# Wider moving operands for two kinds of narrow TensorE products in an attention stage

## The chip, the cores and the metric

The kernel runs on one core of one Trainium2 chip. The metric is the device time of one execution in microseconds. All times and counts below come from the times of the kernel before, from the page of its profile or from an answer of its trace.

## What is computed

Three parts follow one another. An xLSTM-like attention with input, forget and output gates runs over 4 batches, 8 heads, 768 tokens and a head size of 40. Its result, rows of 320 numbers for 3072 tokens, goes to a router that gives each token to one of 8 experts, 384 tokens each. Each expert is a two-layer product with ReLU, followed by a gated product common to all. Cut to what matters here:

```
for t in range(S):                       # attention, per batch and head
    m_new = max(f[t] + m, i[t])
    C = exp(f[t] + m - m_new) * C + exp(i[t] - m_new) * outer(v[t], k[t])
    n = exp(f[t] + m - m_new) * n + exp(i[t] - m_new) * k[t];  m = m_new
    y[t] = sigmoid(o[t]) * (C @ q[t]) / max(abs(n @ q[t]), 1)
logits = x @ w_gate                      # x: 3072 x 320, w_gate: 320 x 8
# tokens to experts by the order of the logits, 384 to each; then
h = relu(x[mask] @ w1[e]); out[mask] = h @ w2[e]
y = (sigmoid(x @ wg) * (x @ wv)) @ wo
```

## The kernel before

The attention is done in 6 chunks of 128 tokens. In a chunk the 32 pairs of batch and head are taken in three sets of 12, 12 and 8 heads. So there are 18 steps j (chunk c = j // 3, set s = j % 3). All products of this stage are in float32, apart from the decays. In the trace a float32 product has two matmul records and two weight loads, a transpose one of each.

The work of a step, by method:

- `trans` transposes queries and keys, 3 heads at a time (line 211); ScalarE copies them out.
- `decay` forms the logarithm of the decay matrix of 4 heads: one bfloat16 product of 512 columns that writes all of a PSUM tile (line 235), then four of 128 columns, each into its quarter of the same tile (line 237). ScalarE takes the exponential (line 241) into `ee`.
- `score` forms keys times queries, 128 columns for each head (line 250), and VectorE multiplies `ee` by them.
- `outp` multiplies these weights by the values: for each head the weights (128 x 128) are loaded as the stationary operand and the head's 41 columns (40 values and a one) are streamed (line 297). The results of all heads of the step stand side by side in one PSUM tile `po`, 41 columns each.
- `inter` and `state` read and renew the running state, three heads at a time with 123 columns (lines 261 and 280). `comb` adds the parts (line 307).
- `flip` transposes the finished rows of two batches (line 341), and `lmm` multiplies them by the router's weights: five accumulated products of 16 columns each (line 354), of which VectorE copies the 16 logits of each token out (`half2`, line 359).

Around this, VectorE, ScalarE, GpSimd and the DMA queue unpack the weights of the last part (`prep_moe2`, lines 745 to 796), from step 2 on. The program gives the stage in the order of the list `ORDER`, but the order of each engine's instructions is then settled by a planner that works with estimated costs of the instructions, so that products of neighbouring steps stand between each other. Behind the attention that planner is off, and the order is the program's.

The router starts when the last logits are there (line 606 is its first product). The experts follow; there TensorE works without pause.

Of the kernel before, what the change touches and what calls it, by code (L numbers as in the profile page):

```python
# [7 lines left out]
FT = mybir.dt.float32  # L8
# [13 lines left out]
L = 128  # L22
# [3 lines left out]
E = 8  # L26
# [4 lines left out]
GK = (3, 3, 2)  # L31
# [9 lines left out]
class Attention:  # L41
# [248 lines left out]
    def outp(self, j, k):  # L290
        nc = self.nc
        s = j % NS
        if k == 0:
            self.PO[j] = self.ps.tile([L, HS, 41], FT, name="po", bufs=1)
        w = self.W.pop((j, k))
        for h in range(4):
            nc.tensor.matmul(self.PO[j][:, 4 * k + h, :], w[:, h, :], self.VN[s][:, 4 * k + h, :], start=True, stop=True)  # L297

    def comb(self, j):
        nc = self.nc  # L300
# [48 lines left out]

    def lmm(self, c, z, i0, n):  # L350
        if i0 == 0:
            self.PL = self.ps.tile([L, 2, E], FT, name="pic", bufs=1)
        for i in range(i0, i0 + n):
            self.nc.tensor.matmul(self.PL, self.XT[c, z][:, i, :], self.wgt[:, i], start=(i == 0), stop=(i == 4))

    def half2(self, c, z, i0=0):
        self.lmm(c, z, i0, 5 - i0)
        lg = self.g["lg"].rearrange("p (b c) e -> p b c e", c=NC)
        self.nc.vector.tensor_copy(lg[:, 2 * z:2 * z + 2, c, :], self.PL)

    def run(self, rt, fn):
        rt.consts(self.one)
# [828 lines left out]
```

## Time and profile before

| | |
|---|---|
| median of 3 runs | 876.02 us (875.86 to 878.23) |
| the profiled execution | 875.33 us |
| its span, first to last instruction | 873.4 us |
| time around the span | 1.93 us |
| TensorE: matmuls busy, weight loads busy | 827.8 us (95%), 788.4 us (90%) |
| VectorE, ScalarE, GpSimd busy | 535.7 us, 377.7 us, 229.0 us |
| mean granted TensorE clock | 0.958 |

The page shows each engine's busy time, then the span in 40 slices with the granted clock of TensorE (1.00 is 2.4 GHz, 0.50 is 1.2 GHz), then the chain of work that ended last and the costliest groups of instructions. Matmuls are pipelined: a run of them that begin 0.1 us apart and last 0.28 us each shows TensorE as busy throughout, so a busy share near 1 does not tell how fast it works. For that, the length of a run of products is to be read against their number.

### The profile page before, as it was taken

Reading aid. Unit: us, or ns where it says so; the run is one execution under the profiler, and the core shown is the slowest. Engines: PE = TensorE matmul, PEld = TensorE weight load, DVE = VectorE, ACT = ScalarE, POOL = GpSimd, SP = SyncE. Lnnn points to the kernel's source line nnn. Section 1 sums busy time; section 2 is a strip of 40 time slices with the busy share of each in tenths; the row PEclk is TensorE's granted clock in tenths of the full one; section 3 lists DMA queues with packets and bytes.
Section 4 is the critical chain, followed back from the end, with each engine's and each line's share of the span. In section 5 each row is a group of like instructions: output and inputs, shape, how many; then the busy total and the mean of one; then the engine's idle time right before and its main releaser. Section 6 shows DMA issues by size and latency. Waiting matters only on the chain.

```text
span 873.4 us, 16420 instructions
## 1 busy us (share of the span) xinstructions
PE 827.8 (95%) x6332; PEld 788.4 (90%) x6332; DVE 535.7 (61%) x1442; ACT 377.7 (43%) x827; POOL 229.0 (26%) x235
## 2 busy tenths in 40 slices
PE   6899898997499999999999999999999999999996
PEld 5899897996299999999999999999999999999996
DVE  8668787875666666565565666566565665643321
ACT  6798889660043252252225134322522342252321
POOL 1125343430120081063017104400810360062001
PEclk9799999897599999999999999999999999999998
DMA  7997786620130230050040005002200500140000
GB/s 131 164 233 176 190 190 155 154 59 31 59 98 1 69 88 24 13 145 23 1 131 26 23 2 156 23 2 78 79 23 2 146 33 2 38 118 23 1 1 24
DMA packets 124574, 64.07 MB, mean 73 GB/s; under 512 B 103760, under 2 KB 115216, under 8 KB 124496
## 3 DMA queue, kind: packets, MB, share of 16 engines
q1 hardware_dynamic: 122048, 55.10, 25.7%
q0 software_dynamic: 2304, 7.87, 2.8%
q8 instruction: 50, 0.82, 0.4%
q14 instruction: 28, 0.23, 0.1%
q10 hardware_dynamic: 144, 0.05, 0.0%
HBM read 55.14 MB, written 7.86 MB: 72 GB/s over the span
## 4 chain that ended last, share of the span: by engine, by line
PE 71%; DVE 2%; DMA 1%; ACT 1%; issue 1%; POOL 0%; POOLq 0%; DVEq 0%; ACTq 0%
PE mm L974 8%; PE mm L975 8%; PE mm L996 8%; PE mm L976 8%; PE ac L1090 5%; PE mm L981 5%; PE mm L980 5%; PE ac L1092 5%; PE ac L1091 5%; PE rp L606 3%; PE ac L1013 3%; PE ac L1015 2%; PE ac L1014 2%; PE ac L1019 1%; PE ac L1018 1%; DMA xg<-xd,ix 1%
## 5 line engine op out<-in xcount | busy, mean ns | idle before, releaser
L974 PE MATMUL mm<-yh,mh 128*128 128x384 f32 x384 | 134.1, 349 | 0.0
L975 PE MATMUL mm<-yh,ml 128*128 128x384 f32 x384 | 129.1, 336 | 0.0
L976 PE MATMUL mm<-yl,mh 128*128 128x384 f32 x384 | 129.1, 336 | 0.0
L934 POOL DMA_INDIRECT xg<-xd,ix x24 | 24.0, 1000 | 376.3 <-DVE scr L701 371.4
L1069 ACT ACTIVATE sg<-mm 128x384 f32<-128x384 f32 x96 | 47.2, 492 | 132.9 <-PE mm L981 132.9
L1076 DVE TENSOR_TENSOR gl<-gf,gh 128x384 fp32r<-128x384 f32 x96 | 77.5, 807 | 37.1 <-ACT gh L1082 36.9
L1082 ACT ACTIVATE gh<-gf 128x384 fp32r<-128x384 f32 x96 | 50.2, 523 | 114.6 <-DVE gf L1081 114.6
L1090 PE MATMUL ac<-oh,gh 128*128 128x320 f32 x288 | 92.6, 321 | 0.0
L1092 PE MATMUL ac<-oh,gl 128*128 128x320 f32 x288 | 89.2, 310 | 0.7 <-DVE gl L1076 0.7
L1091 PE MATMUL ac<-ol,gh 128*128 128x320 f32 x288 | 89.1, 310 | 0.0
L1081 DVE TENSOR_TENSOR gf<-sg,mm 128x384 f32<-128x384 f32 x96 | 52.6, 548 | 52.6 <-ACT sg L1069 52.0
L1004 ACT ACTIVATE gh<-mm 128x384 fp32r<-128x384 f32 x64 | 31.3, 491 | 118.2 <-PE ac L1019 52.8
L974 PEld LDWEIGHTS mm<-yh,mh 128*128 128x128 f32 x384 | 72.4, 189 | 0.2 <-DVE xl L915 0.2
L975 PEld LDWEIGHTS mm<-yh,ml 128*128 128x128 f32 x384 | 72.6, 189 | 0.0
L976 PEld LDWEIGHTS mm<-yl,mh 128*128 128x128 f32 x384 | 72.2, 188 | 0.0
L981 PE MATMUL mm<-pad,mr 128*128 128x384 f32 x192 | 64.7, 337 | 0.0
L980 PE MATMUL mm<-y,m 128*128 128x384 f32 x192 | 64.5, 336 | 0.0
L250 PE MATMUL s<-qT,kb 120*128 120x128 f32 x384 | 59.6, 305 | 3.1 <-ACT kb L219 2.1
L250 PEld LDWEIGHTS s<-qT,kb 120*128 120x128 f32 x384 | 54.1, 216 | 4.5 <-ACT kb L219 2.9
L241 ACT ACTIVATE ee<-pg,GT 128x128 f32<-128x128 f32 x192 | 54.5, 391 | 3.5 <-PE po L297 1.6
L1092 PEld LDWEIGHTS ac<-oh,gl 128*128 128x128 f32 x288 | 54.1, 188 | 0.9 <-DVE gl L1076 0.9
L1090 PEld LDWEIGHTS ac<-oh,gh 128*128 128x128 f32 x288 | 54.5, 189 | 0.0
(287 smaller groups left out, 1990.6 us busy)
## 6 DMA issues: line engine op xcount, KB each, us to landing
ws<-in_moe_w_dram SPq DMA_DIRECT2D x15, 480.0 KB, 6.7
ws<-in_moe_w_dram SPq DMA_DIRECT2D x14, 512.0 KB, 4.1
ws<-in_moe_w_dram SPq DMA_DIRECT2D x18, 256.0 KB, 5.4
on<-in_o_gate_dram SPq DMA_DIRECT2D x24, 160.0 KB, 3.8
xd<-y SPq DMA_DIRECT2D x24, 160.0 KB, 2.5
st<-in_moe_w_out_dram SPq DMA_DIRECT2D x12, 320.0 KB, 3.6
st<-in_moe_w_gate_dram SPq DMA_DIRECT2D x8, 384.0 KB, 4.3
st<-in_moe_w_val_dram SPq DMA_DIRECT2D x8, 384.0 KB, 4.2
```

The costliest lines, as they stand in the source:

```text
L241: nc.scalar.activation(ee[:, h, :], pg[:, h, :], AF.Exp, bias=self.GT[:, c, h0 + h:h0 + h + 1])
L250: nc.tensor.matmul(s[:, h, :], self.KB[:, a, r, :], self.QT[j][:, a, :], start=True, stop=True)
L974: mm(p, wh[:, d, cs], h[:, d], start=(d == 0), stop=False)
L975: mm(p, wl[:, d, cs], h[:, d], start=False, stop=False)
L976: mm(p, wh[:, d, cs], l[:, d], start=False, stop=False)
L980: mm(p, w2[:, cs], x[2], start=False, stop=False)
L981: mm(p, wr[:, c2], self.pad[z], start=False, stop=True)
L996: mm(p, (self.al if t == 1 else self.ah)[:, d, cs], x[t // 2][:, d], start=(d == 0 and t == 0), stop=False)
L1076: nc.vector.tensor_tensor(gl, hs[f - 1][0], hs[f - 1][1].bitcast(FT), op=OP.subtract)
L1090: mm(o, gh[:, ts], self.oh[:, k], start=(k == 0), stop=False)
L1091: mm(o, gh[:, ts], self.ol[:, k], start=False, stop=False)
L1092: mm(o, gl[:, ts], self.oh[:, k], start=False, stop=(k == 11))
```

## The change

In `outp`, each head's weights are multiplied not by that head's 41 columns but by up to three heads' (123 columns; 82 and 41 for the last two heads of a step). The columns of the next heads are written with products that nobody wants, and the next heads' own products, which come after them, write over them. In `lmm`, the 16 columns of the router's weights are streamed seven times (112 columns, by an access with step 0) into a PSUM tile seven times as wide, of which the copy reads the first 16 columns. The number of instructions stays.

```diff
         w = self.W.pop((j, k))
         for h in range(4):
-            nc.tensor.matmul(self.PO[j][:, 4 * k + h, :], w[:, h, :], self.VN[s][:, 4 * k + h, :], start=True, stop=True)
+            hh = slice(4 * k + h, min(4 * k + h + 3, 4 * GK[s]))
+            nc.tensor.matmul(self.PO[j][:, hh, :], w[:, h, :], self.VN[s][:, hh, :], start=True, stop=True)
...
     def lmm(self, c, z, i0, n):
         if i0 == 0:
-            self.PL = self.ps.tile([L, 2, E], FT, name="pic", bufs=1)
+            self.PL = self.ps.tile([L, 7, 2, E], FT, name="pic", bufs=1)
         for i in range(i0, i0 + n):
-            self.nc.tensor.matmul(self.PL, self.XT[c, z][:, i, :], self.wgt[:, i], start=(i == 0), stop=(i == 4))
+            self.nc.tensor.matmul(self.PL, self.XT[c, z][:, i, :], self.wgt[:, i][:, None].to_broadcast([L, 7, 2, E]),
+                                  start=(i == 0), stop=(i == 4))
...
-        self.nc.vector.tensor_copy(lg[:, 2 * z:2 * z + 2, c, :], self.PL)
+        self.nc.vector.tensor_copy(lg[:, 2 * z:2 * z + 2, c, :], self.PL[:, 0])
```

## Rows read from the trace of the kernel before

**Rows 1.** The page, 40 slices of the span: TensorE's busy tenths, its granted clock.

```profile
PE   6899898997499999999999999999999999999996
...
PEclk9799999897599999999999999999999999999998
```

**Rows 2.** Stretches: us, PE, PEld, DVE, ACT, POOL busy (instructions), PEclk, DMA, GB/s.

```profile
33.00:212.00 179.00, 169.25 (x1377) 160.21 (x1377) 132.75 (x289) 137.64 (x370) 63.91 (x65) 0.90 0.68 155
...
236.50:873.40 636.90, 624.75 (x4617) 601.56 (x4617) 357.14 (x978) 216.12 (x404) 156.39 (x147) 0.99 0.16 49
```

**Rows 3.** The same view: the stretches of the attention at the lower clock.

```profile
17.98:21.39 3.41, 3.14 (x17) 2.51 (x17) 3.38 (x8) 3.34 (x11) 0.00 (x0) 0.50 0.30 36
31.64:41.88 10.24, 8.89 (x45) 8.69 (x46) 3.30 (x6) 6.84 (x20) 2.11 (x2) 0.50 1.02 172
65.77:69.18 3.41, 3.41 (x20) 3.07 (x19) 0.74 (x4) 3.39 (x7) 0.98 (x1) 0.50 0.85 237
89.66:93.08 3.42, 3.42 (x18) 3.42 (x18) 1.46 (x3) 3.38 (x12) 2.17 (x3) 0.50 0.83 175
120.38:123.80 3.42, 3.42 (x18) 3.42 (x18) 1.44 (x4) 3.38 (x11) 1.00 (x1) 0.50 1.00 208
147.69:151.10 3.41, 3.41 (x16) 3.25 (x17) 1.96 (x5) 3.41 (x12) 0.26 (x1) 0.50 1.04 225
168.17:175.00 6.83, 6.83 (x34) 6.83 (x34) 6.56 (x17) 2.55 (x9) 2.99 (x3) 0.50 0.56 171
205.72:211.54 5.82, 5.43 (x26) 5.19 (x27) 0.81 (x4) 1.12 (x4) 0.07 (x1) 0.50 0.24 86
```

**Rows 4.** Timeline, TensorE ahead of falls: start, length, line, tiles, shape, count.

```profile
63.79 1.96 PE L297 MATMUL po<-vn,ee 128*128 128x41 f32 x16
...
116.97 2.77 PE L297 MATMUL po<-vn,ee 128*128 128x41 f32 x24
...
164.64 1.88 PE L297 MATMUL po<-vn,ee 128*128 128x41 f32 x16
...
166.70 1.19 PE L354 MATMUL pic<-wgt,xt 128*128 128x16 f32 x10
```

**Rows 5.** Timeline, TensorE after waits (in brackets: idle before, and who ended it).

```profile
32.99 0.90 PE L211 MATMUL tr<-ident,qn 128*120 128x128 f32 x3 [2.30 <-ACT GT L175]
...
88.28 0.49 PE L250 MATMUL s<-qT,kb 120*128 120x128 f32 x2 [0.78 <-ACT kb L219]
...
147.57 1.80 PE L250 MATMUL s<-qT,kb 120*128 120x128 f32 x6 [1.36 <-ACT kb L219]
...
205.85 0.40 PE L354 MATMUL pic<-wgt,xt 128*128 128x16 f32 x1 [0.64 <-ACT xt L342]
```

**Rows 6.** Timeline, VectorE waiting for TensorE at the lower clock.

```profile
36.12 0.67 DVE L310 COPY t<-po 128x492 f32<-128x492 f32 x1 [3.27 <-PE po L297]
...
69.16 0.67 DVE L263 TENSOR_TENSOR t<-pic,GT 128x492 f32<-128x492 f32 x1 [2.67 <-PE pic L261]
...
211.31 0.17 DVE L359 COPY lg<-pic 128x16 f32<-128x16 f32 x1 [2.61 <-PE pic L354]
```

**Rows 7.** Timeline, TensorE: runs of products of different widths, at either clock.

```profile
34.32 1.77 PE L297 MATMUL po<-vn,ee 128*128 128x41 f32 x8
...
42.73 1.04 PE L297 MATMUL po<-vn,ee 128*128 128x41 f32 x8
...
102.09 1.05 PE L261 MATMUL pic<-cs,qT 120*128 120x123 f32 x8
...
175.20 0.38 PE L235 MATMUL pg<-negi,tris 128*128 128x512 bf16 x1
175.42 0.39 PE L237 MATMUL pg<-GB,sel 96*128 96x128 bf16 x4
```

**Rows 8.** Groups, 33 to 212 us: line, engine, shape, count, busy us, mean ns, idle before.

```profile
L297 PE MATMUL po<-vn,ee 128*128 128x41 f32 x344 | 43.5, 281 | 0.1
L261 PE MATMUL pic<-cs,qT 120*128 120x123 f32 x110 | 17.4, 307 | 0.5 <-DVE lg L359 0.5
```

## The prediction, made before the result was known

> **What bounds the kernel now.** I read the slices first, then stretches of the span, then single runs of TensorE. In the slices TensorE is busy nearly throughout, and its granted clock dips again and again in the first ten slices and hardly later [rows 1]. The change touches only the attention, which ends at 212 us; from 236.5 us on the clock is 0.99 [rows 2] and nothing is changed there. In the attention's main part, 33 to 212 us, TensorE shows 169 of 179 us busy, VectorE 133 and ScalarE 138, at a mean clock of 0.90 [rows 2]. So TensorE is the most loaded engine there, and it works part of the time at half rate.
>
> Where, the eight stretches at 0.50 (1.2 GHz) tell [rows 3]. TensorE was busy in them for 3.14 + 8.89 + 3.41 + 3.42 + 3.42 + 3.41 + 6.83 + 5.43 = 38.0 us. That the rate really halves is seen on the same products: eight records of line 297 take 1.77 us at the lower level and 1.04 us at the upper [rows 7]; without the last one's own length (about 0.4 and 0.28 us) they begin 0.20 and 0.11 us apart. So about half of 38.0 us, 19 us, is what the lower level costs TensorE. That TensorE is what others wait for in these stretches shows on VectorE, which stood idle for 3.27, 2.67 and 2.61 us behind it there [rows 6].
>
> What came ahead of the falls is of two kinds. Ahead of those at 65.77, 120.38 and 168.17 us TensorE never paused, but it issued long runs of the narrow products: 16, 24 and 16 records of 41 columns, and ten of 16 columns [rows 4]. Ahead of those at 89.66 and 147.69 us it had waited for ScalarE's copies of the keys, 0.78 and 1.36 us [rows 5]. The falls at 31.64 and 205.72 us had both: 16 narrow records right before, and a wait (2.30 and 0.64 us) beside [rows 5]. The one at 17.98 us lies in the stage's start.
>
> **The change part by part.** *More columns in the same number of products.* A run of 41 columns and one of 123 columns take the same at the upper level: 1.04 us for eight of line 297, 1.05 us for eight of line 261 [rows 7]. Each record stands on its own load of 128 stationary columns, and that load sets the distance of 0.11 us. So 82 more columns at line 297 and 96 more at line 354 lie under a load that is there already; I cost them at nothing. If that cover were gone: 512 bfloat16 columns take 0.22 us from one start to the next [rows 7], 0.43 ns a column, and a float32 product has two records, so 0.86 ns. Added are 6 x (2 x (10 x 82 + 41) + 6 x 82 + 41) = 13,530 columns of values and 60 x 96 = 5,760 of logits, together 19,290 columns or 16.6 us. The row of 123 columns is of the very width, so I take zero and keep 16.6 us for a rival.
>
> The Trainium skill, page "TensorE: Matmul & The Clock Gate", section "Back-to-back issue gap", speaks against this change: there the spacing of matmuls grows with the columns streamed. By that rule alone the added columns would lengthen every product, and the sum would be worse by the 16.6 us; lines 297 and 261 differ by a factor of three in columns and not in pace, so this trace goes by the load instead.
>
> *A longer way to the last result.* A record lasts 281 ns on average at 41 columns and 307 ns at 123 [rows 8]. The last head of a step keeps its 41 columns, so `comb` waits no longer; the 12 groups of logits end later by about 0.03 us each. At most one such delay lies on the path for each of the 48 groups of `outp` and 12 of logits: 60 x 0.026 = 1.6 us; most of them are behind other work, and I take 0.5 us.
>
> *Writing over the next heads' columns.* Products that write the same PSUM region follow each other on one engine. Line 235 writes a whole tile and line 237 writes parts of it again 0.22 us later, though the first lasts 0.38 us [rows 7]: no wait lies between. I cost it at zero; were there one, each product of line 297 would start after the end of the one before, 0.28 instead of 0.11 us [rows 7, 8]. The values of the next heads belong to the same step and were loaded with the others two steps ahead.
>
> *The clock.* If narrow runs are what lets it fall, the falls go where such runs stand ahead. For the three without a wait, half of 3.41 + 3.42 + 6.83 us [rows 3] is 6.8 us of TensorE's time. Not all of it reaches the end: in 168.17 to 175.00 us VectorE is busy for 6.56 of 6.83 us and in the two others ScalarE for 3.39 and 3.38 us [rows 3], so one of them is soon late instead, and TensorE will wait for it as it does now before lines 250 [rows 5]. I take two thirds, 4.5 us; the bounds are zero and 6.8. For the falls at 31.64 and 205.72 us the product time is half of 8.89 and of 5.43 us, 7.2 us together. TensorE is plainly the bound in both [rows 6], and behind the second comes the router, which can start only after the last logits; but the waits ahead of them stay, so that a fall may stay too. Again two thirds, 4.8 us, between zero and 7.2. At 17.98 us I count nothing: whatever is gained is lost in the 2.30 us wait for the gates' exponential at 32.99 us [rows 5], which comes from VectorE's chain. The falls at 89.66 and 147.69 us I leave.
>
> *The planner.* It will see dearer products and can order the stage anew. The trace of before shows nothing of the new order. Its waits are 0.64 to 2.30 us each [rows 5]; one such of 0.64 us more or less in each of the 16 steps after the second would be 10 us either way. As neither sign has a reason, I take zero and widen the range.
>
> The sum is 4.5 + 4.8 - 0.5 = 8.8 us. From the profiled execution's 875.33 us (873.4 us of span and 1.93 us around it) this leaves 866.5 us. The median of the runs is 0.7 us higher than the profiled one, so I forecast 867.2 us, about 1.0% less. A measurement of this kernel can tell some 0.3% (2.6 us) from no change.
>
> **The rivals.** (1) *Only the three falls without a wait go.* The waits of [rows 5] then let the clock fall as before. This gives 876.0 - 4.5 + 0.5 = 872 us. For it speaks that two falls have waits and hardly a narrow product ahead; against it, that as long a wait stands at 31.64 us beside 16 narrow records, which now are wide. (2) *The new order costs more than the clock gives.* The place is the queue of TensorE: if `score` products come later behind `outp`, VectorE gets its weights later, and TensorE waits in the next `outp`. One more wait of the size of [rows 5] in each step is 0.64 x 16 = 10 us, and the time 877 us; the worst of them, 1.36 us, gives 22 us and 889 us. It decides from 0.55 us a step on, where the 8.8 us are eaten. Against it speaks that dearer products leave the planner nearer to what the chip does, where the widths make no difference of pace. (3) *The columns are paid for.* 16.6 us more and 9.3 us of clock back: 883 us. The equal runs of 41 and 123 columns [rows 7] speak against it. (4) *The clock does not care for columns*: all falls stay, and the time is 876 to 877 us. For it speaks that weight loads keep TensorE as busy in narrow runs as in wide ones; against it, that three falls come with no pause at all.
>
> The same page of the Trainium skill, in its table of goals, ties a throttled clock to idle gaps between bursts of matmuls, which is rival 4 (or 1 for the falls with a wait); the three falls behind unbroken narrow runs disagree with it.
>
> **How the numbers follow.** Forecast 0.58 (861 to 871 us by itself, from the bounds of the two thirds and half of the planner's 10 us below); rival 1: 0.17; rival 2: 0.14; rival 3: 0.04; rival 4: 0.07. The range runs from 860.5 us, where nearly all 14.0 us come through and the order helps a little, to 877 us, which takes in rivals 1 and 4 and the mild side of rival 2. Faster than 873.4 us: all of the forecast and 0.12 of rival 1, 0.70. Within 0.3%: the rest of rival 1, rival 4 and a part of rival 2, 0.15. Slower: rival 3 and most of rival 2, 0.15.
>
> **What would show it.** In the changed kernel's windows, no stretch at 0.50 behind runs of line 297 or 354, and a mean clock of the main part of 0.95 or more. Runs of eight 123-column records of line 297 in 1.05 us; 1.8 us at the upper clock would make step one wrong. The last logits earlier by 7 to 10 us, and an unchanged distance from there to the end. If TensorE's waits grow by more than 5 us, the two thirds were too much, or the planner's order decided.

## The result

The changed kernel takes 866.94 us (866.39 to 868.64, four runs) against 875.94 us (875.83 to 878.23) of the kernel before: a ratio of 0.9894, with a 95% interval of 0.9873 to 0.9916, or 9.0 us less. The forecast was 867.2 us. The same program, timed once more in the series of the last experiments, gave 866.66 us and a ratio of 0.9905 (0.9876 to 0.9934).

The profiled execution of the changed kernel is the slowest of its four, 868.64 us with a span of 866.6 us. So the two profiles stand 6.7 us apart and not 9. The second profile of the same program took 866.23 us with a span of 864.2 us; both are used below.

The page of the changed kernel, TensorE's busy tenths and its granted clock in 40 slices, to be held against [rows 1]:

```profile
PE   6899897995599999999999999999999999999996
...
PEclk9999998997599999999999999999999999999999
```

Stretches of the changed kernel, columns as in [rows 2]: its only stretch at the lower clock before the last logits, and its main part:

```profile
135.94:142.76 6.82, 5.50 (x27) 5.08 (x27) 0.82 (x3) 6.76 (x21) 1.99 (x2) 0.50 0.21 54
33.00:205.00 172.00, 156.57 (x1374) 147.20 (x1374) 131.09 (x287) 137.14 (x369) 65.24 (x63) 0.98 0.70 160
```

Of the eight stretches of [rows 3], with 38.0 us of TensorE's busy time, none is left; one of 5.50 us is new. The mean clock of the main part went from 0.90 to 0.98. TensorE's busy time there fell from 169.25 us [rows 2] to 156.57 us, that is by 12.7 us; VectorE's and ScalarE's hardly moved (132.75 to 131.09 us, 137.64 to 137.14 us).

The timeline of VectorE, the copies of the last logits in the changed kernel's first and second profile (the line of the copy moved with the edit, and by another line in the second):

```profile
204.93 0.17 DVE L362 COPY lg<-pic 128x16 f32<-128x16 f32 x1 [1.67 <-PE pic L356]
```

```profile
203.44 0.17 DVE L361 COPY lg<-pic 128x16 f32<-128x16 f32 x1 [1.67 <-PE pic L355]
```

Before, the last copy began at 211.31 us after a wait of 2.61 us [rows 6]. So the logits are there 6.4 and 7.9 us earlier. From there to the end it is 873.4 - 211.3 = 662.1 us before and 661.7 and 660.8 us after: what lies behind the attention is unchanged but for 0.4 and 1.3 us, whose cause is open.

What the regained time met is told by TensorE's waits from 33 us to the last logits (line waited for: us in total, times, longest), before and after:

```profile
PE tr L211 <- ACT GT L175: 2.3, 1, 2.3
PE s L250 <- ACT kb L219: 2.1, 2, 1.4
PE tr L341 <- DVE y L325: 1.8, 3, 0.8
PE pic L280 <- DVE t L263: 1.0, 1, 1.0
...
PE pg L235 <- ACT ee L241: 0.5, 2, 0.3
```

```profile
PE pic L280 <- DVE t L263: 4.8, 4, 1.9
PE pg L235 <- ACT ee L241: 3.2, 4, 1.8
PE pic L261 <- DVE cs L285: 1.6, 1, 1.6
PE tr L211 <- ACT GT L175: 1.2, 1, 1.2
```

TensorE's time without a product in the main part went from 179.0 - 169.25 = 9.8 us (up to 212 us) to 172.0 - 156.57 = 15.4 us (up to 205 us). So nearly 6 of the 12.7 us came back as waits. The two that grew most are line 280's for VectorE's reading of the `pic` buffer (1.0 to 4.8 us) and line 235's for ScalarE's exponentials (0.5 to 3.2 us).

The new stretch at the lower clock, from 135.94 us on, begins behind one such wait and within the next, which ends at 137.26 us, in the timeline of TensorE:

```profile
134.54 0.90 PE L261 MATMUL pic<-cs,qT 120*128 120x123 f32 x6 [1.65 <-DVE cs L285]
137.26 0.58 PE L235 MATMUL pg<-negi,tris 128*128 128x512 bf16 x1 [1.82 <-ACT ee L241]
```

The changed products themselves, by shape (as in [rows 8], 33 to 205 us):

```profile
L299 PE MATMUL po<-vn,ee 128*128 128x123 f32 x276 | 36.9, 277 | 0.0
L356 PE MATMUL pic<-wgt,xt 128*128 128x112 f32 x120 | 16.0, 277 | 0.8 <-ACT xt L344 0.6
...
L299 PE MATMUL po<-vn,ee 128*128 128x82 f32 x34 | 6.0, 258 | 0.0
L299 PE MATMUL po<-vn,ee 128*128 128x41 f32 x34 | 5.9, 260 | 0.0
```

### The profile page after: what moved, and what is told of

Its sections match the earlier page's. It is cut to its first block, busy times and chain, and to the rows that moved or that the text cites. A ratio compares the mean times of both kernels' runs of the same rounds, so it can differ in the third digit from the quotient of the medians.

```text
span 866.6 us, 16410 instructions
## 1 busy us (share of the span) xinstructions
PE 816.2 (94%) x6332; PEld 775.3 (89%) x6332; DVE 534.0 (62%) x1442; ACT 376.9 (43%) x827; POOL 230.4 (27%) x235
## 4 chain that ended last, share of the span: by engine, by line
PE 72%; DVE 2%; DMA 1%; ACT 0%; issue 0%; POOL 0%; POOLq 0%; ACTq 0%; DVEq 0%
PE mm L977 8%; PE mm L999 8%; PE mm L978 8%; PE mm L979 8%; PE mm L984 5%; PE mm L983 5%; PE ac L1093 5%; PE ac L1095 5%; PE ac L1094 5%; PE rp L609 3%; PE ac L1016 3%; PE ac L1018 3%; PE ac L1017 3%; PE ac L1022 1%; DMA xg<-xd,ix 1%; PE ac L1021 1%
## 5 line engine op out<-in xcount | busy, mean ns | idle before, releaser
L250 PE MATMUL s<-qT,kb 120*128 120x128 f32 x384 | 54.6, 287 | 2.3 <-DVE ee L251 1.2
L1094 PEld LDWEIGHTS ac<-ol,gh 128*128 128x128 f32 x288 | 54.3, 188 | 0.0
```

Source lines behind the costliest of these rows:

```text
L250: nc.tensor.matmul(s[:, h, :], self.KB[:, a, r, :], self.QT[j][:, a, :], start=True, stop=True)
L1094: mm(o, gh[:, ts], self.ol[:, k], start=False, stop=False)
```

## Experiments

The theory (A) was that runs of narrow products let TensorE's clock fall, that the added columns are free, and that only a part of the regained time reaches the end. The rivals were that the planner's new order made the gain (B) and that the clock falls behind waits alone (C).

### Each half of the change

```diff
 e_values: outp streams hh (three heads) as in the change; lmm as before
 e_logits: lmm streams its 16 columns seven times as in the change; outp as before
```

> Only the products with values are widened (123 columns); the logits keep their 16. Theory A (runs of narrow products let TensorE's clock fall, the added columns are free, about half of the regained TensorE time reaches the end): most falls go, since the long narrow runs are those with values; 867 to 871 us, mean clock 0.97 or more. Rival B (the gain is the planner's new order, not the clock): the order is a third one, so the time may lie anywhere between 866 and 878 us without regard to the clock's mean. Rival C (the clock falls behind waits alone): the clock's mean stays near 0.958 and what time is gained is order alone.

> Only the logits are widened (112 columns); the products with values keep their 41. Theory A: the falls behind 16 and 24 records of 41 columns stay, one or two of them go where ten records of 16 columns made up the rest; the end of the attention gains some 2 us because its last 20 products run at the upper level; 872 to 875 us, mean clock 0.96 to 0.965. Rival B: anywhere between 866 and 878 us. Rival C: as before, 876 us.

Measured: values alone 870.09 us, ratio 0.9939 (0.9920 to 0.9959); logits alone 873.68 us, ratio 0.9983 (0.9966 to 1.0001). The kernel with wide values has in its attention one stretch at the lower clock, and the end of it, in which the last narrow logits stand:

```profile
71.97:75.38 3.41, 3.41 (x19) 3.13 (x18) 3.41 (x8) 3.16 (x8) 1.00 (x1) 0.50 0.64 149
201.67:205.32 3.65, 3.45 (x18) 3.22 (x17) 0.34 (x2) 0.87 (x2) 0.00 (x0) 0.50 0.13 45
```

Both times lie in theory A's ranges, but the 1.8 us of the logits alone are not clear of noise. The mean clock of the two profiles is 0.978 and 0.972, against 0.958 before, so rival C's forecast of an unchanged mean fails; the 0.972 is also above theory A's 0.96 to 0.965.

Theory A missed something else with the logits alone: the falls behind 16 and 24 records of 41 columns were to stay. Four stretches at the lower clock are left before the last logits (from 33.80, 74.76, 105.48 and 143.03 us on). Each begins in a wait of TensorE or at most 1.5 us behind one (waits of 1.96, 0.46, 3.06 and 2.31 us). So no fall without a wait is left there, though the values are still narrow; whether that is due to the wide logits or to the new order this pair does not tell.

Each of the two kernels has an order of its own by the planner, so they do not exclude that the order has a share. The whole change is better than the values alone by some 3 us. Of that the last logits show 0.2 us in the first profile of the changed kernel and 1.7 us in the second (205.16 us with the values alone, against 204.93 and 203.44 us); the rest is left open.

### The order held still

With the planner off in the attention, the order on every engine is the program's. The instructions and their order are then the same for narrow and wide products, and only the columns differ.

```diff
+    ctx.enter_context(tc.manual_schedule())
     with ExitStack() as c2:
         at = Attention(c2, tc, g, a, xd)
...
-    ctx.enter_context(tc.manual_schedule())
```

> The kernel before with the planner off in the attention too, so that every engine's order is the program's. Together with the next kernel this holds the order still: the two have the same instructions in the same order on every engine and differ in the columns alone. The order written in the program is probably worse than the planner's: 880 to 910 us under every theory. Theory A expects falls of the clock behind runs of narrow products here as well; rival C only behind waits.

> The changed kernel with the planner off in the attention too. Theory A: 5 to 12 us below the kernel with narrow products in the same order, with a higher mean clock, since nothing else differs. Rival B (order): within 2 us of it. Rival C (waits): within 2 us of it, with the same stretches at the lower level.

Measured: 935.26 us (1.0681, 1.0632 to 1.0730) and 915.91 us (1.0464, 1.0426 to 1.0501): 19.4 us from the columns alone, more than theory A's 12. Stretches up to the last logits, narrow and wide:

```profile
0.00:272.70 272.70, 219.73 (x1548) 204.00 (x1549) 155.03 (x381) 155.81 (x417) 64.66 (x81) 0.82 0.57 119
```

```profile
0.00:251.70 251.70, 188.07 (x1548) 173.06 (x1549) 155.25 (x381) 154.19 (x417) 64.81 (x81) 0.95 0.62 129
```

The same 1548 records make TensorE busy for 31.7 us less, at a mean clock of 0.95 instead of 0.82, and the last logits come 21.0 us earlier. No order can have done this, which is what rival B needs; and since TensorE's time without a product is no shorter (53.0 us narrow, 63.6 us wide), rival C falls too. The program's order is some 60 us slower than the planner's with narrow products and 49 us with wide ones, worse than the 880 to 910 us expected.

### Values alone, and two heads, in that order

```diff
 e_man_values: as e_man_wide, but lmm streams its 16 columns once
 e_man_82:     as e_man_wide, with
+            hh = slice(4 * k + h, min(4 * k + h + 2, 4 * GK[s]))
```

> The order of the program on every engine, with only the products with values widened; to be read against the pair e_man_narrow (935.3 us) and e_man_wide (915.9 us), which have the same order. Theory A (the clock follows the streamed columns, the values being most of the narrow ones): two thirds or more of the 19.4 us, 916 to 922 us, with the lower level left mainly where the last logits stand. If the logits were the larger part, 928 to 932 us.

> The order of the program on every engine, logits widened, products with values streaming two heads (82 columns) instead of three. Between e_man_narrow (935.3 us, 46.7 us of half of TensorE's busy time at the lower level) and e_man_wide (915.9 us, 9.3 us). Theory A (the clock follows the streamed columns): between them, 918 to 928 us, unless 82 columns are already enough for the clock, then within 2 us of e_man_wide.

Measured: 927.93 us for the values alone, only 7.3 of the 19.4 us, outside theory A's range; 920.78 us with 82 columns and wide logits, in its range. Why the logits count for so much here is seen at one of their groups. In this order it stands behind a wait of TensorE for VectorE, of 1.8 us in each of three kernels. TensorE's timeline with all products narrow (`e_man_narrow`), with narrow logits alone (`e_man_values`) and with all wide (`e_man_wide`):

```profile
126.16 1.16 PE L250 MATMUL s<-qT,kb 120*128 120x128 f32 x8 [1.79 <-DVE ee L251]
127.15 1.73 PE L354 MATMUL pic<-wgt,xt 128*128 128x16 f32 x10
...
130.81 1.77 PE L297 MATMUL po<-vn,ee 128*128 128x41 f32 x8
```

```profile
122.09 1.16 PE L250 MATMUL s<-qT,kb 120*128 120x128 f32 x8 [1.80 <-DVE ee L251]
123.09 2.07 PE L355 MATMUL pic<-wgt,xt 128*128 128x16 f32 x10
...
127.08 1.91 PE L298 MATMUL po<-vn,ee 128*128 128x123 f32 x8
```

```profile
118.74 1.16 PE L250 MATMUL s<-qT,kb 120*128 120x128 f32 x8 [1.79 <-DVE ee L251]
119.74 1.27 PE L355 MATMUL pic<-wgt,xt 128*128 128x112 f32 x10
...
121.94 1.05 PE L298 MATMUL po<-vn,ee 128*128 128x123 f32 x8
```

The stretches at 0.50 that begin at the logits of the first two, and the same place in the third, which stays at 1.00:

```profile
127.61:141.26 13.65, 13.65 (x70) 12.76 (x70) 5.22 (x16) 5.94 (x19) 2.79 (x3) 0.50 0.81 148
```

```profile
123.18:130.01 6.83, 6.83 (x37) 6.22 (x36) 3.53 (x11) 3.48 (x10) 0.54 (x1) 0.50 1.16 209
```

```profile
118.74:125.57 6.83, 6.83 (x63) 6.59 (x64) 4.35 (x13) 4.09 (x13) 1.64 (x2) 1.00 1.04 193
```

Behind waits of the same length the clock fell 0.5 and 0.1 us into the narrow logits and did not fall at the wide ones, and the fall lasted 13.65 us where the values behind it were narrow too and 6.83 us where they were wide. So narrow products do not only go ahead of falls: behind a wait they go with a fall that wide ones are spared, and with a longer one the more of them there are. At the group of logits before this one, where the waits differ (1.80, 3.23 and 3.17 us), the stretches are 13.65, 10.24 and 3.41 us long. The wide values that stand in the second kernel's stretch are slowed with the rest (1.91 against 1.05 us for eight).

### More columns than the load covers

```diff
 e_man_246: as e_man_wide, with
+            hh = slice(4 * k + h, min(4 * k + h + 6, 4 * GK[s]))
```

> As e_man_wide in the same order, but six heads (up to 246 columns) are streamed with each head's weights. If added columns are free at any width, or a record streams its columns once at 0.43 ns (246 columns, 106 ns, under the 112 ns of a load): within 3 us of e_man_wide's 915.9 us. If a record takes its columns twice (0.86 ns a column, 0.21 us for 246), TensorE has some 22 us more work in the attention, of which half or more reaches the end: 925 to 938 us, and the products with values stand 0.21 us apart at the upper level.

Measured: 928.45 us, in the range of columns that are taken twice, and 12.5 us slower than with 123 columns in spite of a mean clock of 0.97 up to the last logits. TensorE's timeline in this kernel and in e_man_wide, eight records each at a granted clock of 1.00, and the stretch up to the last logits of the former:

```profile
65.73 1.76 PE L298 MATMUL po<-vn,ee 128*128 128x246 f32 x8
...
0.00:264.30 264.30, 207.64 (x1548) 188.03 (x1549) 155.34 (x381) 154.85 (x417) 64.97 (x82) 0.97 0.59 122
```

```profile
71.81 1.05 PE L298 MATMUL po<-vn,ee 128*128 128x123 f32 x8
```

Without the last record's own 0.38 us, records of 246 columns begin (1.76 - 0.38) / 7 = 0.20 us apart, 0.80 ns a column: a float32 record takes its columns about twice as long as the 0.43 ns a column of the bfloat16 product in [rows 7]. TensorE is busy for 207.64 - 188.07 = 19.6 us more. By that pace 123 columns are estimated at 0.10 us, just under the 0.11 us from one record to the next in [rows 7].

### Where the rest of the regained time went

With the unpacking of the last part's weights moved behind the attention, in the program's order, the pair of narrow and wide was profiled again, in one execution each. These kernels are longer in all; only their last logits are read.

```diff
-                self.step(j, lambda n: [next(side, 0) for _ in range(n)])
+                self.step(j, lambda n: None)
```

> As e_man_narrow, with the unpacking of the last part's weights moved from between the attention's steps to behind them (longer in all, by that work). To be read is the time of the last logits alone, against the next kernel. Both theories: some lower-level stretches behind narrow runs; the last logits earlier than e_man_narrow's 272.7 us, by 20 to 60 us.

> The same with the wide products. In the pair with the unpacking between the steps, 37 us of TensorE's time at the lower level were regained and the last logits came 21.0 us earlier (56%). If the unpacking on VectorE and ScalarE is what takes the rest, the share rises here to 75% or more of what is regained. If the attention's own chain takes it (exponentials on ScalarE, the products with them on VectorE, two buffers of PSUM each), it stays at 45 to 65%.

Measured: up to the last logits, narrow and wide:

```profile
0.00:228.70 228.70, 189.67 (x1548) 176.91 (x1549) 110.22 (x285) 132.29 (x369) 32.82 (x49) 0.91 0.49 92
```

```profile
0.00:218.30 218.30, 180.01 (x1548) 167.85 (x1549) 110.06 (x285) 132.04 (x369) 32.80 (x49) 0.97 0.51 95
```

By the measure of the expectation, half of TensorE's busy time in the lower stretches went from 15.6 to 3.1 us and the last logits came 10.4 us earlier: 83%, where it was 56% with the unpacking between the steps. By busy time, 9.7 us less against 31.7 us less, the shares are all of it and two thirds. VectorE has 45 us less to do here. TensorE's largest wait from 60 to 215 us, for the scores' product with the weights on VectorE, in the narrow and wide kernel with the unpacking and then in the narrow and wide one without:

```profile
PE s L250 <- DVE ee L251: 14.0, 7, 4.5
```

```profile
PE s L250 <- DVE ee L251: 18.1, 8, 4.5
```

```profile
PE s L250 <- DVE ee L251: 3.1, 4, 1.3
```

```profile
PE s L250 <- DVE ee L251: 2.8, 4, 1.1
```

With the unpacking between the steps this wait grows when TensorE gets faster (14.0 to 18.1 us); without it, it is short and does not grow (3.1 to 2.8 us). That speaks for the unpacking as what takes a part of what does not reach the end, in this order. It is not shown for all of it: the wait's 4.1 us are less than half of the 31.7 - 21.0 = 10.7 us, and the second pair has a third as much to regain, with its falls in other places.

### A second buffer where the changed kernel waits

```diff
 e_wide_again: the changed kernel itself
 e_pic2_tr1:   all tiles pic bufs=2, all tiles tr of the attention bufs=1
 e_pic2_s1:    all tiles pic bufs=2, tile s bufs=1
```

> The changed kernel once more, so that the next two can be held against it on the same chip: 866 to 869 us, ratio to before 0.987 to 0.993.

> The changed kernel with two PSUM buffers for the products of state, old state and logits (tile pic) and one instead of two for the transposes (tile tr), the PSUM being full. In the changed kernel TensorE's largest waits are those of line 280 for VectorE's read of the one pic buffer (4.8 us, 1.0 before) and of 261 for the old state (1.6 us). If the single pic buffer is what takes back the regained time: 2 to 5 us faster than the changed kernel. If VectorE and ScalarE are late anyway with the unpacking between the steps, or the single transpose buffer costs as much: within 2 us, or slower.

> The same with the second buffer taken from the scores (tile s). If the pic buffer is the cause and the scores' second buffer is not needed: 2 to 5 us faster than the changed kernel. The scores are read by VectorE in the middle of every step, so that more likely TensorE waits there: 3 to 15 us slower.

Measured: 866.66, 901.07 and 884.38 us; the last two have ratios of 1.0290 (1.0241 to 1.0339) and 1.0104 (1.0073 to 1.0135). TensorE's waits from 33 to 225 us with one buffer for the transposes:

```profile
PE pg L235 <- ACT ee L241: 14.5, 9, 4.5
PE s L250 <- ACT kb L219: 7.8, 7, 2.0
...
PE pic L280 <- DVE t L263: 0.5, 1, 0.5
```

The wait of line 280 is gone (4.8 to 0.5 us), but lines 235 and 250 wait for ScalarE for 22.3 us, where it was 4.3 us in the changed kernel. So with a buffer taken from the transposes the kernel is 34 us slower than the changed one, and with one taken from the scores 18 us, where 3 to 15 us were expected. The planner orders each of these kernels anew, and the times hold that too. Whether a second `pic` buffer is worth something when no other tile gives one up is not shown. Neither kernel beats the changed one.

## Why the prediction was right, point by point

**The bound.** Right. TensorE's busy time in the attention fell, VectorE's and ScalarE's hardly moved, and the end came earlier.

**The columns at nothing.** Right for this width, with the price of the rival mis-sized. Eight records of values take 1.05 us at 123 columns (`e_man_wide`), 1.04 us at 41 [rows 7], and line 299 begins without idle time. But the price if uncovered was taken from a bfloat16 product as 0.43 ns for each of two records; a float32 record takes 0.80 ns (`e_man_246`). Rival 3's 16.6 us should have been 0.80 / 0.43 as much, about 31 us, and by the same estimate the cover is nearly used up: 0.10 of 0.11 us.

**The later last result and the overwriting.** Nothing speaks against either: the records are 277 ns long at 123 columns and 260 ns at 41, less than the 26 ns of the forecast apart, and no wait lies ahead of line 299.

**The clock.** The mechanism is right: in the same order of instructions, wider columns alone raise the clock and give 19.4 us. The sizes in the sum are another matter: the number came out better than its terms.

The regained time was forecast as 14.0 us of TensorE's time, from five falls. By busy time it was 12.7 us in the main part, and it came about otherwise. All eight falls went, not five: those at 17.98, 89.66 and 147.69 us did not come again, and one came new at waits. Which waits TensorE meets is up to the order, so single falls at waits can't be carried over from one trace to the next. On the other side, halving the busy time overstates a fall's price: by [rows 7] eight records take 1.77 and 1.04 us, 41% less, and their starts are 0.20 and 0.11 us apart, 45% less, not 50%.

Of the regained time less came through than two thirds. The last logits came 6.4 us earlier in the first profile, half of 12.7 us, and 7.9 us in the second, three fifths of 13.0 us (156.00 us busy from 33 us to its last logits, 169.03 us before). The forecast had 9.3 us and named 7 to 10 us as a sign. By its other sign, waits that grow by more than 5 us, the two thirds were too much: TensorE's idle time grew by nearly 6 us. That the medians differ by 9.0 us, as the sum of 8.8 us had it, is partly luck: the first pair of profiles is 6.7 us apart, and the 9.1 us of the second pair hold 1.3 us from behind the attention, which the sum did not count. The forecast's bounds of 861 to 871 us do not follow from what it names for them either: with all 14.0 us and 5 us for the order the lower one would be 876.0 - 14.0 + 0.5 - 5 = 857.5 us.

**The absorber.** The forecast named VectorE and ScalarE as soon late. Right: the waits for VectorE's line 263 and ScalarE's line 241 grew. In the program's order the unpacking takes a part of the rest; for the planner's order no run shows what delays the two engines.

**The planner, and rival 2.** The term was set at zero with 10 us either way. With the planner off, the change gives 19.4 us, so the gain needs no new order. How much the new order adds to or takes from the 9 us stays open: no run has the planner's old order with the wide products.

**Rivals 1 and 4.** Rival 1 fell, as the time is 5 us below its 872 us and the falls at 31.64 and 205.72 us went too; the wait at the first of them was shorter this time (2.3 to 1.2 us), so that fall alone would not have settled it. Rival 4 fell with the pair in one order, and so did the reading of the table of goals in the Trainium skill's page "TensorE: Matmul & The Clock Gate" by which idle gaps alone throttle. Waits do matter beside: the remaining fall of the changed kernel begins behind a wait of 1.65 us and within one of 1.82 us, with products of 123 columns before it.

## What to carry to other kernels

A product whose pace is set by the load of its stationary operand has room for more streamed columns at no cost until they need as long as the load (here 123 columns were free and 246 were not), and in a kernel whose TensorE clock falls behind runs of such products, filling that room can be worth the time of the falls. Read the room from two runs of the same type and different widths, not from another data type. Count as gain what the next engine lets through, and look for the widths of products behind waits too, since here narrow ones made a wait end in a fall and a fall last longer.

## What was not expected of the hardware

A float32 record of 246 columns takes 0.20 us at the upper clock, 0.80 ns a column, while a bfloat16 product takes 0.43 ns. In one order of instructions and behind waits of 1.8 us, the clock stayed at the lower level for 13.65 us where logits and values were narrow and for 6.83 us where only the logits were, and it did not fall where both were wide.
